# Raw weights loaded ahead, value products issued in blocks, and nine early tiles transposed on TensorE

## The chip, the core and the metric

The kernel runs on one core of a Trainium2 chip. Its engines work side by side, each through its own queue in order: TensorE (PE; its weight loads are listed as PEld), VectorE (DVE), ScalarE (ACT), GpSimd (POOL) and SyncE (SP), which here issues every DMA. The metric is the device time of one execution in microseconds (us); lower is better.

## The reference

The reference is attention in which a query only sees keys of its own cluster, and a feed-forward network behind it.

```
q, k, v: (4, 8, 768, 64)    centroids: (8, 16, 64)    out: (3072, 512), float32
q_assign = argmax(normalized q . normalized centroid)        # the same for k
mask     = q_assign[:, :, :, None] == k_assign[:, :, None, :]
scores   = where(mask, q @ k.T / sqrt(64), -1e9)
attn     = softmax(scores);   x = attn @ v  -> (3072, 512)
h        = max(x @ w1, x @ w2, x @ w3)                       # w: 512 x 768
out      = h @ w_out                                         # 768 x 512
```

The four weights come as float64, seen as pairs of 32-bit words, or as four 16-bit words each.

## The kernel before

**Precision.** Operands of the large matmuls are split into two float16 parts, high and low, and a product is the sum of three float16 products. Powers of two scale each operand first.

**Attention.** There are 4 batches, 8 heads in 4 pairs, and 6 tiles of 128 queries; 192 tiles of 128 queries x 768 keys in all, called steps here. A visit is one batch, one pair and three query tiles: six steps. `scores` does one step: four matmuls into a PSUM tile `big` (three buffers; L482 the product of q and k, L484 the cluster part), a minimum on DVE that also gives the row's extreme (L487), the exponential on ACT (L490), a cast to the high half (L493), a subtract for the low half (L495; on POOL at odd steps, on DVE at even ones), and a transposing DMA of both halves `hl` into `pt` (L496). After the six steps of a visit `av` multiplies by the values: it forms the reciprocals of the row sums, spreads them by small matmuls (L510) and makes 36 products of 64 columns (L514), two at a time side by side in the array, then scales and splits the result (L522 to L529).

**Preparation.** Before a pair's first step, `prep_units` loads q and k (L360), scales and splits them, finds the cluster of each row, and moves parts between partitions by DMA (L405 to L407, L463). `v_prep` scales (L330 in the first batch) and splits the values (L340, L341).

**Weights.** `w_units` (w1, w2, w3; six column blocks of three loads) and `wo_units` (w_out, six loads) bring in 24 raw pieces of 512 KB. In each, `convert` loads into one of two raw buffers `wd` (L195), casts the top 16 bits on ACT (L197) and merges the rest on DVE (L199). `hold` first writes one element of the raw buffer on POOL, out of the last step's row sum (L120), so the load can't start earlier. Maxima, scales (`pow2_scale`, L106) and the split (L208 to L210) follow.

**Feed-forward.** For each three query tiles of a batch, once all four pairs are there: `hidden` (18 units of 12 matmuls, L555) and `outp` (three units of 18 matmuls, L589).

**Order.** Every unit gets a priority, counted in steps; a scheduler that works with simulated times then sets each engine's order, taking what is ready with the lowest number. `spread` deals units over a stretch of steps; `behind` queues a unit behind the last instruction of a kind on its engine. Numbers below 0 in `W_LATE` and the like put a unit ahead of the step it is filed under.

## Time and profile before

| | |
|---|---|
| median of three runs | 871.94 us (867.68 to 874.14) |
| the profiled execution | 872.91 us, span 871.1 us |
| mean granted TensorE clock | 0.923 |
| busy: PE, DVE, ACT, POOL | 729.3, 559.7, 463.1, 450.4 us |
| DMA queue q1 | 71.5% of the 16 engines' span |
| transposing DMAs | 192, 4.0 us from issue to landing (median) |

A line such as `L495 POOL TENSOR_TENSOR hl<-e,hl` names the line of the kernel, the engine, the operation, and the tile written and those read. "x96 | 159.0, 1656" is the count, the busy time in us and the mean length in ns. A chain of waits is followed back from the last instruction, at each step to what released it. The granted clock is the share of full speed that TensorE had.

### The profile page before, as it was taken

To read this page: it belongs to the slowest core of one execution; us is meant where nothing else is said; L and a number is where in the kernel's file an instruction comes from. 1 tells how busy PE (TensorE), PEld (TensorE's weight loads), DVE (VectorE), ACT (ScalarE), POOL (GpSimd) and SP (SyncE) were. 2 spreads that over 40 slices of the span, in tenths; PEclk is the share of its full clock that TensorE was granted. 3 is DMA by queue.
4 is the path that set the end of the run, shared out by engine and by line. 5 is a ranking of instruction groups with operands and counts; after the bars stand their busy time and mean duration, and the time that the engine had idled before them with its cause. 6 is when DMAs were issued, how large, how long until landed. Compare 5 with 4: busy or idle time off the path is not lost.

```text
span 871.1 us, 13288 instructions
## 1 busy us (share of the span) xinstructions
PE 729.3 (84%) x4629; PEld 391.6 (45%) x4629; DVE 559.7 (64%) x1169; ACT 463.1 (53%) x827; POOL 450.4 (52%) x464
## 2 busy tenths in 40 slices
PE   2035374788868989999789999997999999999997
PEld 0012132344434545555444555454545554555563
DVE  7663877786897867547686686368768663556110
ACT  2545467654663646646554656464556465566201
POOL 1166355658585565337655745266666652354221
PEclk9976566689888999999999999999999999999999
DMA  6176869986786778768888978597986976666300
GB/s 230 36 169 140 201 143 214 203 182 139 178 204 128 171 167 154 138 117 165 170 157 201 188 139 142 113 180 144 189 194 128 156 136 134 112 118 110 91 1 36
DMA packets 329154, 128.90 MB, mean 148 GB/s; under 512 B 304384, under 2 KB 315520, under 8 KB 329088
## 3 DMA queue, kind: packets, MB, share of 16 engines
q1 hardware_dynamic: 329088, 128.06, 71.5%
q8 instruction: 36, 0.59, 0.3%
q14 instruction: 30, 0.25, 0.1%
HBM read 31.49 MB, written 6.29 MB: 43 GB/s over the span
## 4 chain that ended last, share of the span: by engine, by line
PE 45%; DVE 18%; POOL 11%; DMA 10%; issue 9%; ACT 5%; SPq 1%; POOLq 0%; DVEq 0%; ACTq 0%
PE one L555 17%; PE one L589 11%; PE big L514 7%; DVE big L487 4%; PE big L482 4%; PE big L484 3%; POOL hl L495 3%; DMA pt<-hl 2%; DMA stage<-in_qk_dram 2%; PE big L510 2%; DMA wd<-in_moe_w_dram 2%; DMA wd<-in_moe_w_out_dram 2%; POOL qk L399 2%; DMA stage<-in_v_dram 2%; DVE hl L495 2%
## 5 line engine op out<-in xcount | busy, mean ns | idle before, releaser
L487 DVE TENSOR_SCALAR_CACHE_REDUCE big<-big,nsc 128x768 f32<-128x768 f32 x192 | 194.2, 1017 | 78.3 <-PE big L484 77.1
L495 POOL TENSOR_TENSOR hl<-e,hl 128x768 f16<-128x768 f32 x96 | 159.0, 1656 | 148.9 <-ACT hl L493 147.3
L555 PE MATMUL one<-x,w16a 128*128 128x384 f16 x1152 | 208.1, 330 | 5.1 <-DVE vf_h L567 3.7
L490 ACT ACTIVATE big<-big,nm 128x768 f32<-128x768 f32 x96 | 83.8, 873 | 146.3 <-DVE big L487 130.9
L555 PEld LDWEIGHTS <-w16a 128*128 128x128 f16 x1152 | 111.1, 98 | 90.0 <-issue 21.1
L482 PE MATMUL big<-qk 128*128 128x512 f16 (+1 forms) x384 | 105.9, 357 | 48.5 <-DVE hl L495 14.0
L514 PE MATMUL big<-pt,v 128*64 128x384 f16 x1152 | 129.8, 341 | 2.4 <-DMA pt<-hl 2.4
L490 ACT ACTIVATE e<-big,nm 128x768 f32<-128x768 f32 x96 | 86.5, 901 | 71.3 <-DVE big L487 56.4
L495 DVE TENSOR_TENSOR hl<-big,hl 128x768 f16<-128x768 f32 x96 | 91.4, 952 | 41.8 <-ACT hl L493 39.6
L555 PE MATMUL one<-x,w16b 128*128 128x384 f16 x576 | 108.3, 340 | 6.7 <-DVE vf_h L567 5.2
L484 PE MATMUL big<-qk 96*128 96x512 f16 (+1 forms) x384 | 106.5, 357 | 6.9 <-DVE qk L465 4.3
L514 PEld LDWEIGHTS <-v 128*64 128x64 f16 x1152 | 71.8, 114 | 50.9 <-issue 26.0
L482 PEld LDWEIGHTS <-qk 128*128 128x128 f16 x384 | 35.6, 102 | 104.8 <-issue 67.2
L493 ACT CAST hl<-e 128x768 f16<-128x768 f32 x96 | 80.1, 834 | 2.4 <-DMA pt<-hl 0.6
L555 PEld LDWEIGHTS <-w16b 128*128 128x128 f16 x576 | 57.5, 101 | 51.3 <-issue 17.5
L493 ACT CAST hl<-big 128x768 f16<-128x768 f32 x96 | 76.6, 798 | 2.0
L528 POOL TENSOR_SCALAR x<-xs 128x384 f16<-128x384 f32 x32 | 16.4, 512 | 99.3 <-DVE xs L524 83.8
L484 PEld LDWEIGHTS <-qk 96*128 96x128 f16 x384 | 40.4, 105 | 40.0 <-issue 9.2
L589 PE MATMUL one<-wo,wf_h 128*128 128x512 f16 x216 | 56.0, 381 | 0.8 <-ACT o L598 0.8
L589 PE MATMUL one<-wo,vf_h 128*128 128x512 f16 x216 | 51.8, 380 | 2.7 <-DVE vf_h L567 2.4
L367 DVE TENSOR_REDUCE q_m<-stage 128x1 f32<-128x768 f32 x32 | 30.2, 948 | 33.9 <-DMA stage<-in_qk_dram 33.8
L399 POOL TENSOR_TENSOR qk<-stage,qk 128x768 f16<-128x768 f32 x30 | 49.6, 1667 | 3.1 <-ACT qk L398 2.9
(150 smaller groups left out, 892.5 us busy)
## 6 DMA issues: line engine op xcount, KB each, us to landing
stage<-in_qk_dram SPq DMA_DIRECT2D x32, 384.0 KB, 5.0
wd<-in_moe_w_dram SPq DMA_DIRECT2D x18, 512.0 KB, 4.8
out_dram<-o SPq DMA_DIRECT2D x24, 256.0 KB, 2.5
qk<-qk SPq DMA_DIRECT2D x15, 384.0 KB, 4.3
qk<-qk SPq DMA_DIRECT2D x30, 192.0 KB, 3.4
stage<-in_v_dram SPq DMA_DIRECT2D x12, 384.0 KB, 4.6
pt<-hl SPq DMA_TRANSPOSE x192, 4.0
wd<-in_moe_w_out_dram SPq DMA_DIRECT2D x6, 512.0 KB, 4.5
```

The source lines that it names most:

```text
L367: nc.vector.tensor_reduce(m2[:, i : i + 1], x, axis=AX.X, op=ALU.max, apply_absolute_value=True)
L399: last["lo"] = nc.gpsimd.tensor_tensor(t[:, AQ, i], x, t[:, BQ, i], op=ALU.subtract)
L482: nc.tensor.matmul(t[:, lo:hi], aq[:, qs], ak[:, lo:hi], start=True, stop=False)
L484: last["pe"] = nc.tensor.matmul(t[:, lo:hi], bq[0:K2, qs], bk[0:K2, lo:hi], start=False, stop=True)
L487: last["nm"] = nc.vector.tensor_scalar(e, e, nsc[b, h // 2], 3.0e38, op0=ALU.mult, op1=ALU.min, accum_out=nm)
L490: nc.scalar.activation(x, e, AF.Exp, bias=nm, scale=-1.0, accum_out=r)
L493: nc.scalar.copy(hl[:, 0, :], x)
L495: eng.tensor_tensor(hl[:, 1, :], x, hl[:, 0, :], op=ALU.subtract)
L510: nc.tensor.matmul(t[D * i : D * i + D, at : at + P], w, ident, start=True, stop=True)
L514: nc.tensor.matmul(t[D * i : D * i + D, 0:NB], v[:, i, kt, a], pts[i][:, :, c * QT + kt, :], start=(n == 0), stop=(n == len(parts) - 1),)
L555: nc.tensor.matmul(t[:, 0:NB], w16[jt // JA][:, jt % JA, wa, i, ct], x16[b, gi, ct][:, xa, :], start=(n == 0), stop=(n == 3 * CT - 1),)
L589: nc.tensor.matmul(t[:, 0:DM], h16[jt][:, ha, tt * P : (tt + 1) * P], wo16[0][:, jt, wa, :], start=(n == 0), stop=(n == 3 * JT - 1),)
```

## The change

It has four parts.

1. **Loads apart from conversions.** `convert` becomes `w_load` and `w_convert`. `pace` and `hold` go, and with them the POOL copies. The 24 pieces are dealt 1.9 steps apart: piece n is loaded at step k - 1 and converted at step k + 1, with k = 2 + 1.9 (n - 2); the first two are loaded ahead of step 0. Each such unit is queued behind the last L487, L490 and L496 on their engines. Before, 18 pieces were spread over steps 0 to 37 and six over 33 to 47, with load and conversion together.
2. **TensorE transposes.** At steps 0, 3, ..., 24 the transposing DMA gives way to twelve TensorE transposes through a float16 identity into two PSUM tiles `one`; ACT copies the high half's result into `pt`, DVE the low half's.
3. **Value products as blocks.** `av` is cut in three: the sums (`av_sums`), the 36 products, and the split (`x_split`). The products get a priority six steps below that of the other two.
4. **Preparation.** The first two values' loads stand ahead of step 0, apart from their maxima; pairs 2 and 3 of the first batch are prepared over steps 2 to 7 and 7 to 13 (before: 4 to 9 and 10 to 15).

```diff
-    def convert(wp, src, a, d):
-        n = d.shape[-1]
+    def w_load(wp, src, a, n):
         x = wp.tile([P, n + 1, 4], I16, tag="wd", name="wd", bufs=2)
-        hold(x[0:1, 0, 0:2].bitcast(F32))
         xf = x.rearrange("p n w -> p (n w)")
         nc.sync.dma_start(out=xf[:, 1 : 1 + 4 * n].rearrange("p (a m) -> p a m", a=a), in_=src)
+        return x
+
+    def w_convert(x, d):
+        n = d.shape[-1]
...
+        last["exp"] = nc.scalar.activation(x, e, AF.Exp, bias=nm, scale=-1.0, accum_out=r)
...
+        if not by_pe:
+            last["dma"] = nc.sync.dma_start_transpose(out=pt[:, g], in_=hl.rearrange("p a s -> p (a s)"))
+            return
+        for a in range(2):
+            o = one().bitcast(F16)[:, 0:S]
+            for c in range(QT):
+                nc.tensor.transpose(o[:, c * P : (c + 1) * P], hl[:, a, c * P : (c + 1) * P], identh)
+            d = pt[:, g, a * QT : (a + 1) * QT, :].rearrange("p c q -> p (c q)")
+            if a:
+                nc.vector.tensor_copy(d.bitcast(I16), o.bitcast(I16))
+            else:
+                nc.scalar.copy(d.bitcast(I16), o.bitcast(I16))
...
+    def paced(step, u, keys=("nm", "exp", "dma"), late=-2):
+        def f():
+            with ExitStack() as st:
+                for k in keys:
+                    if k in last:
+                        st.enter_context(tc.issue_after(last[k].ins))
+                u()
+        plan.setdefault(max(int(step // 1), 0), []).append((step + late, f))
...
+    W_STEP = 1.9
+    for n in range(24):
+        k = 2 + (n - 2) * W_STEP
+        if n >= 2:
+            paced(k - 1, (wl + ol)[n])
+        paced(max(k + 1, 0.5), (wc + oc)[n])
+        if n < 18 and n % 3 == 2:
+            for i, u in enumerate(wu[n // 3][2]):
+                paced(k + 2 + i, u)
+    paced(47, w_common)
+    spread([lambda u=u: behind("nm", u) for u in prep_units(0, 2)], 2, 7, -4)
+    spread([lambda u=u: behind("nm", u) for u in prep_units(0, 3)], 7, 13, -4)
...
-                at_prio(step, scores, b, h, gi * G + g, pt, g, rs, by_pool(step))
+                at_prio(step, scores, b, h, gi * G + g, pt, g, rs, by_pool(step), step < 26 and step % 3 == 0)
...
-        u = lambda a=(b, pr, gi, pts, rs): behind("pe", av, *a)
-        plan.setdefault(step + AV_LAG - 1, []).append((step + AV_LATE, u))
+        k = step + AV_LAG - 1
+        plan.setdefault(k, []).extend(
+            [
+                (k + 1, lambda a=(b, pr, gi, rs): behind("pe", av_sums, *a)),
+                (k - 5, lambda a=(b, pr, gi, pts): behind("pe", av, *a)),
+                (k + 1, lambda a=(b, pr, gi): x_split(*a)),
+            ]
+        )
```

How this moves instructions is seen on three engines. First TensorE about step 74, where the output matmuls of the first feed-forward block stand (`one<-wo,wf_h`), beside value products (`big<-pt,v`). Before:

```order
L510 MATMUL big<-ident,rs 64x128
L589 LDWEIGHTS wf_h
L589 MATMUL one<-wo_1015,wf_h 128x512
L514 LDWEIGHTS v_2390
L514 MATMUL big<-pt,v_2390 64x384
L589 LDWEIGHTS wf_h
L589 MATMUL one<-wo_1015,wf_h 128x512
L514 LDWEIGHTS v_2390
L514 MATMUL big<-pt,v_2390 64x384
```

After, where the products are L541, the output matmuls L619 and the row sums L533:

```order
L619 LDWEIGHTS wf_h
L619 MATMUL one<-wo_1156,wf_h 128x512
L533 MATMUL big<-ident,rs 64x128
L541 LDWEIGHTS v_2505
L541 MATMUL big<-pt,v_2505 64x384
L541 LDWEIGHTS v_2505
L541 MATMUL big<-pt,v_2505 64x384
L541 LDWEIGHTS v_2505
L541 MATMUL big<-pt,v_2505 64x384
```

Before, ten products alternate with output matmuls and 26 follow in a row; after, all 36 stand in a row.

Second ScalarE between the exponentials of steps 1 and 2 (`vf` and `v` are the values, `stage` and `qk` the q and k of the next pair). Before:

```order
L490 ACTIVATE e,rs<-big,nm 128x768
L493 CAST hl<-e 128x768
L330 ACTIVATE vf<-vf,s_v_301 128x768 x2
L397 ACTIVATE stage<-stage,q_s 128x768 x2
L330 ACTIVATE vf<-vf,s_v_301 128x768 x2
L340 CAST v_337<-vf 128x12x64
L340 CAST v_406<-vf 128x12x64
L398 CAST qk<-stage 128x768 x2
L340 CAST v_621<-vf 128x12x64
L340 CAST v_827<-vf 128x12x64
L490 ACTIVATE big,rs<-big,nm 128x768
```

After, with L503 for the exponential, L505 for the cast of the high half, L519 for the copy of a transposed tile, L195 for the cast of a raw weight, L410 and L411 for q and k:

```order
L503 ACTIVATE e,rs<-big,nm 128x768
L519 COPY pt<-one 128x768
L505 CAST hl<-e 128x768
L195 CAST top<-wd 128x512
L410 ACTIVATE stage<-stage,q_s 128x768 x2
L411 CAST qk<-stage 128x768 x2
L503 ACTIVATE big,rs<-big,nm 128x768
```

The eight instructions on the values have gone from here; they now stand behind step 4's.

Third POOL some steps later (`hl<-e` is the low half of an odd step, `wf` and `w16a` belong to the weights, `cl_t` to the clusters). Before:

```order
L120 COPY wd<-rs 1x1
L495 TENSOR_TENSOR hl<-e,hl 128x768
L440 TENSOR_TENSOR cl_t<-cl_t 128x24x16
L120 COPY wd<-rs 1x1
L445 TENSOR_TENSOR cl_t<-cl_t,cl_m 128x24x16
L528 TENSOR_SCALAR x_531<-xs 128x384
L529 TENSOR_TENSOR x_531<-xs,x_531 128x384
L120 COPY wd<-rs 1x1
L495 TENSOR_TENSOR hl<-e,hl 128x768 x2
```

After:

```order
L507 TENSOR_TENSOR hl<-e,hl 128x768
L208 TENSOR_TENSOR w16a<-wf,w16a 128x512
L453 TENSOR_TENSOR cl_t<-cl_t 128x24x16
L208 TENSOR_TENSOR w16a<-wf,w16a 128x512
L507 TENSOR_TENSOR hl<-e,hl 128x768
L458 TENSOR_TENSOR cl_t<-cl_t,cl_m 128x24x16
L507 TENSOR_TENSOR hl<-e,hl 128x768
L558 TENSOR_SCALAR x_602<-xs 128x384
L559 TENSOR_TENSOR x_602<-xs,x_602 128x384
```

The copies into `wd` are gone; the rest stands in a like order.

More of the change, by code (lines that the diff above doesn't have):

```diff
@@ L84 @@
     nc.gpsimd.tensor_copy(ident16, ident)
+    identh = cpool.tile([P, P], F16, name="identh")
+    nc.gpsimd.tensor_copy(identh, ident)
     rank = cpool.tile([P, C], F32, name="rank")
@@ L112, in pow2_scale @@
         return p, s
-    pace = []
-    def hold(x):
-        if pace:
-            nc.gpsimd.tensor_copy(x, pace[-1])
     last = {}
@@ L243, in split, with load, f @@
             return f
-        return [load(i) for i in range(3)] + [scale] + [split(i) for i in range(3)]
+        return [load(i) for i in range(3)], [conv(i) for i in range(3)], [scale] + [split(i) for i in range(3)]
     def wo_units(fp):
         got = []
+        raw = {}
+        def load(jt):
+            def f():
+                w = w_out.bitcast(I16)[jt * P : (jt + 1) * P, :]
+                raw[jt] = w_load(fp[0], w.rearrange("p (a n) -> p a n", a=1), 1, DM)
+            return f
         def part(jt):
             def f():
-                wp = fp[0]
-                w = w_out.bitcast(I16)[jt * P : (jt + 1) * P, :]
                 if jt % 3 == 0:
-                    got[:] = [wp.tile([P, 3 * DM], F32, tag="wf", name="wf", bufs=2)]
+                    got[:] = [fp[0].tile([P, 3 * DM], F32, tag="wf", name="wf", bufs=2)]
                 x = got[0][:, jt % 3 * DM : (jt % 3 + 1) * DM]
-                convert(wp, w.rearrange("p (a n) -> p a n", a=1), 1, x)
+                w_convert(raw.pop(jt), x)
                 row = worow[:, jt : jt + 1]
@@ L283, in common @@
             wsc["w"], wsc["o"] = pw, po
-        return [part(jt) for jt in range(JT)] + [common]
+        return [load(jt) for jt in range(JT)], [part(jt) for jt in range(JT)], common
     vmax = cpool.tile([P, B, NPAIR], F32, name="vmax")
@@ L308, in v_max_first, with load @@
     def v_max_first():
+        def load(i):
+            x = v_first[i] = fp[0].tile([P, 2 * S], F32, tag="vf", name="vf", bufs=2)
+            h = H // 2
+            nc.sync.dma_start(out=x, in_=vv[0, :, i * h : (i + 1) * h].rearrange("p h t d -> p (h t d)"))
         def part(i):
             def f():
-                x = v_first[i] = fp[0].tile([P, 2 * S], F32, tag="vf", name="vf", bufs=2)
-                h = H // 2
-                nc.sync.dma_start(out=x, in_=vv[0, :, i * h : (i + 1) * h].rearrange("p h t d -> p (h t d)"))
+                x = v_first[i]
                 nc.vector.tensor_reduce(
@@ L321, in sc @@
             vsc[0] = pow2_scale(vmax[:, 0, 0:2], "v0")
-        return [part(0), part(1), sc]
+        return [lambda: load(0), lambda: load(1), part(0), part(1), sc]
     v16 = {}
@@ L473, with scores @@
     SCALE = 1.0 / D**0.5
[L477 removed]
+    def scores(b, h, qt, pt, g, rs, by_pool, by_pe):
         aq, bq, bk, ak = (qkt[b, h // 2][:, j, h & 1] for j in range(4))
@@ L495, in scores, with av_sums @@
         eng.tensor_tensor(hl[:, 1, :], x, hl[:, 0, :], op=ALU.subtract)
-        last["dma"] = nc.sync.dma_start_transpose(out=pt[:, g], in_=hl.rearrange("p a s -> p (a s)"))
+        if not by_pe:
[10 more added lines that the diff above has]
+                nc.scalar.copy(d.bitcast(I16), o.bitcast(I16))
     x16 = {}
-    def av(b, pr, gi, pts, rs):
-        v = v16[b, pr]
-        t = big()
+    av_out = {}
+    def av_sums(b, pr, gi, rs):
+        t = av_out[b, pr, gi] = big()
         nc.scalar.activation(rs, rs, AF.Copy, bias=1.0e-9)
```

50 lines of the change are left out of this document (25 added, 25 removed).

## The prediction

> **What bounds the kernel now.** I read the page's head first, then the busy time by stage, then the chain of waits, then single stretches of TensorE's timeline.
>
> ```profile
> span 871.1 us, 13288 instructions
> PE 729.3 (84%) x4629; PEld 391.6 (45%) x4629; DVE 559.7 (64%) x1169; ACT 463.1 (53%) x827; POOL 450.4 (52%) x464
> ```
>
> The profiled execution took 872.9 us, its span is 871.1, so 1.8 us lie around it. It is 1.0 us above the median of the three runs, 871.9. TensorE is the fullest engine, but 84% is a mean over unlike stages. In the stage view the columns are the stretch, its length, busy time with instruction counts for PE, PE's weight loads, DVE, ACT and POOL, then the granted TensorE clock, the share of the DMA engines and GB/s:
>
> ```profile
> 0.00:65.00 65.00, 13.71 (x48) 5.04 (x49) 44.69 (x98) 28.18 (x45) 19.71 (x44) 0.92 0.55 146
> 65.00:109.00 44.00, 19.85 (x98) 8.69 (x99) 26.83 (x59) 22.40 (x38) 23.50 (x24) 0.58 0.75 169
> 109.00:183.00 74.00, 51.89 (x299) 26.72 (x299) 54.25 (x104) 50.91 (x92) 41.45 (x50) 0.67 0.90 193
> 183.00:257.00 74.00, 58.62 (x347) 31.96 (x346) 62.21 (x140) 40.99 (x72) 55.62 (x57) 0.88 0.76 168
> 257.00:452.00 195.00, 179.83 (x1183) 97.40 (x1183) 134.48 (x297) 105.68 (x191) 107.44 (x99) 0.97 0.78 153
> 452.00:636.00 184.00, 175.47 (x1158) 95.03 (x1158) 124.14 (x264) 106.33 (x194) 104.18 (x97) 0.98 0.81 161
> 636.00:805.00 169.00, 168.66 (x1139) 93.50 (x1138) 103.82 (x199) 99.29 (x182) 85.44 (x80) 1.00 0.73 136
> ```
>
> The first four rows hold the first 48 of the 192 score tiles ("steps"); the next three hold 48 each. From 257 us on TensorE is busy 92, 95 and nearly 100% of the time: there TensorE's own work is the bound. Before 257 us it is busy 144.1 of 257 us, at a clock of 0.58 to 0.92, and no engine is full: DVE has 188.0 us (44.69 + 26.83 + 54.25 + 62.21), the DMA engines reach 0.90 in one stage. So the front is bound by waits between engines. The chain of waits of those 257 us names them:
>
> ```profile
> by line: issue 10.5%; DMA wd<-in_moe_w_dram 6.4%; DMA wd<-in_moe_w_out_dram 6.2%; DVE big L487 4.8%; DVE wf L199 4.4%; DMA pt<-hl 4.0%; PE one L555 3.8%; POOL w16a L210 2.6%; DMA stage<-in_v_dram 2.5%; DVE q_m L367 2.4%; DMA qk<-qk 2.1%; PO
> ...
> 53.72 5.08 DMA wd<-in_moe_w_dram
> ...
> 242.21 6.15 DMA wd<-in_moe_w_out_dram
> ```
>
> Loads of raw weights (wd) are 6.4 + 6.2 = 12.6% of 257 us, 32.4 us in seven pieces, of which the first and the last stand above. In each the load has only just been issued when the cast that needs it comes up in ScalarE's queue (waited time, count, longest):
>
> ```profile
> ACT top L197 <- DMA wd<-in_moe_w_dram: 21.5, 12, 5.3
> ...
> ACT top L197 <- DMA wd<-in_moe_w_out_dram: 10.9, 5, 5.7
> ```
>
> **Raw weights ahead.** Before, load and conversion are one unit, and a one-element copy on POOL holds the load back. After, the plan puts the load two steps ahead of its cast. A step of the front lasts 257/48 = 5.4 us, so two last 10.7, and a load lands in 4.8 us at the median:
>
> ```profile
> wd<-in_moe_w_dram SPq DMA_DIRECT2D x18, 512.0 KB, 4.8
> pt<-hl SPq DMA_TRANSPOSE x192, 4.0
> L120 POOL COPY wd<-rs x22: 173/173/645, 52.0 to 238.6; 1x1 f32<-1x1 f32 x22
> ```
>
> So the 32.4 us of weight waits should leave the chain; the 22 POOL copies (22 x 0.17 = 3.8 us of POOL) go too, counted at nothing. The load now waits in the SP queue itself for one of two raw buffers, with the tile transposes queued behind it and, behind those, the value products. I price that at nothing: the conversion that frees the buffer is due 2.8 steps (15 us) earlier and is a cast and a merge of about 1 us each. Were this cover gone, each load would hold the queue for what the conversion is late, at worst the 4 to 6 us of a present piece.
>
> What is late next is DVE. It gets nine more copies, transposed tiles out of PSUM. The nearest row is its subtract over the same 128x768:
>
> ```profile
> L495 DVE TENSOR_TENSOR hl<-big,hl 128x768 f16<-128x768 f32 x96 | 91.4, 952 | 41.8 <-ACT hl L493 39.6
> L493 ACT CAST hl<-e 128x768 f16<-128x768 f32 x96 | 80.1, 834 | 2.4 <-DMA pt<-hl 0.6
> L495 POOL TENSOR_TENSOR hl<-e,hl 128x768 f16<-128x768 f32 x96 | 159.0, 1656 | 148.9 <-ACT hl L493 147.3
> L106 PE MATMUL one<-ident,sc_m 128*128 128x128 bf16 x20 | 4.8, 238 | 12.7 <-DVE sc_m L104 9.2 <-DVE vf_h L567 3.5
> ```
>
> 9 x 0.95 = 8.6 us, so DVE has 196.6 us to do. The fullest stage of the front shows DVE at 62.21/74 = 84%; at that share everywhere the front takes 196.6/0.84 = 234 us, 23 less than 257. The 32.4 us therefore do not all arrive: I take 23. The bounds are 0 (DVE, POOL and the preparation of q and k keep their gaps) and 32.4 + 10.3 (the 4.0% of waits for tile transposes as well).
>
> **Transposes on TensorE.** Steps 0, 3, ..., 24. Off the queues: 9 of 48 transposes of the front, each 4.0 us from issue to landing, in stages where the DMA engines are at 0.55 to 0.90. On TensorE: 9 x 12 = 108 matmuls of 128 columns; L106 gives at most 0.238 us each, 25.7 us in all, 2.9 a tile. TensorE is idle 97.5 of the first 183 us, so this is beside other work, unless it stands in the way: TensorE works in order, and the second six transposes of a tile wait for its low half, made by POOL (1.66 us) on four of the nine tiles and by DVE on five. The scores of the next steps stand behind. The order puts one or two steps' scores between a tile and its transposes, which hides most of it. I take 0.5 us a tile, 4.5 in all, between 0 and the full 0.83 + 1.66 + 2.86 = 5.4 us (cast, subtract, transposes) a tile. ScalarE's nine copies (9 x 0.83 = 7.5 us) lie in its 114.5 idle us of the front and count nothing; without that cover they cost those 7.5. The front: -23 + 5 = -18 us.
>
> The Trainium skill prices the transposes otherwise: "TensorE: Matmul & The Clock Gate", Part 4 (PE-mode transpose), has about 275 ns for one of 128x128 in a kernel; an estimate by it is 108 x 0.275 = 29.7 us, still less than the idle time, and the sum stays.
>
> The preparation of pairs 2 and 3 moves two to three steps earlier, and the scaling of the values on ScalarE and POOL moves from ahead of step 2 to behind step 4. The latter is now on the chain:
>
> ```profile
> 39.99 1.65 ACT vf L330 x2
> 41.64 0.73 ACT v L340
> 42.37 0.07 issue
> 42.44 2.18 POOL v L341 x2
> ```
>
> It must still be done before the first value products, so I count 0, between a gain of the 4.6 us shown and a loss of as much.
>
> **Value products in blocks.** In the late stages, where TensorE is the bound, the products L514 and the output matmuls L589 alternate. In this timeline the columns are start, length, instruction, count:
>
> ```profile
> 366.22 1.67 PE L589 MATMUL one<-wo,wf_h 128*128 128x512 f16 x7
> 367.83 0.43 PE L510 MATMUL big<-ident,rs 128*64 128x128 f32 x2
> ...
> 368.51 0.35 PE L514 MATMUL big<-pt,v 128*64 128x384 f16 x1
> 368.80 0.39 PE L589 MATMUL one<-wo,wf_h 128*128 128x512 f16 x1
> ...
> 374.53 2.30 PE L514 MATMUL big<-pt,v 128*64 128x384 f16 x26
> 376.77 0.34 PE L555 MATMUL one<-x,w16a 128*128 128x384 f16 x1
> ```
>
> Ten of each, alternating, take 374.53 - 368.51 = 6.02 us. Unmixed, seven L589 go from 366.22 to 367.83, 0.23 each, and 26 L514 from 374.53 to 376.77, 0.086 each: two products fill two halves of the array's columns (128*64) and run as a pair, and alternating breaks the pairs. Ten of each would take 3.16 us, so one alternation costs 0.286 us. Over the whole program the order has 50 places where an L514 follows an L589, all past step 48, and 4 after the change: 46 x 0.286 = 13.2 us. That is TensorE time where TensorE is full, so I count all of it, -13; the bounds are 0 and 13.2.
>
> The sum: 872.9 - 18 - 13 = 842 us for an execution like the profiled one, 841 against the median.
>
> **The rivals.** *Nothing in the front.* Preparation chains through DVE and POOL take over at once where the weight waits stood: 859 us. For it: in the fourth stage DVE is at 84% and POOL at 75%. Against: the first three stages are much emptier. 17%.
>
> *Transposes hold TensorE.* Scores queue behind a tile's low half and its twelve transposes; the full 5.4 us on nine tiles are 48 us, 872 - 31 + 48 = 889. It decides from 31/9 = 3.4 us beyond my sum a tile. For it: POOL's low half is the slowest piece of a tile (1.66 us). Against: at most three score tiles are in flight in PSUM, so scores far ahead could not have started anyway. 9%.
>
> *The clock stays up.* A fuller front raises the granted clock. 13.71, 19.85, 51.89 and 58.62 us of matmuls at 0.92, 0.58, 0.67 and 0.88 would be 110.5 at full clock, 33.6 less; half of it on the path is 17, so 824. For it: the clock is 1.00 where TensorE is full. Against: TensorE still idles nearly half of the front. 10%.
> The same part of that page of the Trainium skill says that transposes do not count as busy for the clock; by that rule 108 transposes would not help. No run here shows it yet.
>
> *Given back.* The front shortens, but a chain through the tile transposes, loads and POOL in the middle stages (DMA share 0.78 to 0.81) sets the pace and the time stays at 872. Against: TensorE at 92% and above there. 7%.
>
> **How the numbers follow.** My forecast has 57%: 841. About 1% (8.7 us) is what a measurement can tell from no change. Faster by more: 57 + 10 + 13 of the 17 of "nothing in the front" (859 is 1.5% off, near the line) = 80%; within 1%: 7 + 4 = 11%; slower: 9%. The range goes from 820, the clock's case with some more of the 10.3 us of transpose waits, to 864, the case with nothing in the front with some margin; what lies outside is the slower case, "given back" and little more.
>
> **What would show it.** In the changed profile the weight loads should be gone from the first 257 us' chain, and step 48 should start near 239 us, not 257 (wrong if above 252). DVE's share of the front should rise to about 80%. The alternating stretch should be one block of L514 of about 3 us; TensorE's busy time after the front should fall by some 13 us. If scores in the first 26 steps wait for low halves, or DVE and ScalarE wait for transposes, by more than 2 us a tile, the second rival is at work; a clock above 0.8 between 65 and 183 us would speak for the third.

## The result, and the profile after

The changed kernel takes 876.24 us (875.18 to 877.63), the kernel before in the same comparison 871.4 us (867.68 to 875.18). The ratio is 1.0056, with a 95% interval of 1.0040 to 1.0072: slower by half a per cent, where 841 us were predicted. Its profiled execution has a span of 874.9 us, against 871.1 before:

```profile
span 874.9 us, 13464 instructions
PE 726.0 (83%) x4737; PEld 402.7 (46%) x4737; DVE 564.1 (64%) x1178; ACT 466.2 (53%) x836; POOL 448.1 (51%) x443
```

TensorE does 108 matmuls more (the transposes) in 3.3 us less, and the span grows all the same: idle time is what increased. The stage view of the changed kernel, with the same columns as in the prediction; step 48 starts at 247.4 us (the start of the 49th minimum on DVE), and the last three rows hold 48 steps each:

```profile
0.00:65.00 65.00, 18.27 (x75) 8.04 (x75) 44.42 (x104) 31.08 (x48) 19.88 (x46) 0.83 0.52 150
65.00:109.00 44.00, 26.98 (x159) 14.16 (x160) 31.66 (x66) 27.84 (x49) 28.97 (x25) 0.66 0.71 167
109.00:183.00 74.00, 53.69 (x359) 30.88 (x356) 52.43 (x106) 48.78 (x87) 38.74 (x37) 0.77 0.72 158
183.00:247.40 64.40, 50.08 (x322) 28.89 (x321) 54.15 (x129) 39.08 (x70) 49.86 (x45) 0.92 0.78 170
247.40:444.30 196.90, 174.87 (x1159) 97.26 (x1159) 136.94 (x293) 105.04 (x192) 105.72 (x97) 0.95 0.76 152
444.30:635.50 191.20, 173.53 (x1158) 96.00 (x1158) 126.26 (x262) 104.46 (x191) 104.31 (x96) 0.97 0.79 153
635.50:808.60 173.10, 167.19 (x1152) 94.20 (x1151) 108.92 (x209) 100.47 (x185) 87.36 (x81) 0.99 0.75 136
```

The front did get shorter: 247.4 against 256.6 us, -9.2 where -18 was predicted. The three stages behind it got longer: 196.9, 191.2 and 173.1 us, against 195, 184 and 169 in the prediction's rows. TensorE, nearly 100% busy in the last of them before, is at 97%, and its granted clock is 0.95, 0.97 and 0.99 where it was 0.97, 0.98 and 1.00. The whole part behind step 48, before and then after, in one row each of the same view:

```profile
256.60:871.10 614.50, 585.20 (x3841) 319.15 (x3840) 372.08 (x776) 321.06 (x583) 310.56 (x293) 0.98 0.71 139
```

```profile
247.40:874.90 627.50, 576.98 (x3829) 320.76 (x3828) 381.49 (x778) 319.47 (x583) 310.64 (x291) 0.98 0.70 136
```

TensorE's busy time falls by 8.2 us (585.20 to 576.98). Its idle time, the length less the busy time, rises from 29.3 to 50.5 us. That is +13.0 us, where -13 was predicted. With the front's -9.2 it gives the +3.8 us of the spans.

In the front's chain of waits the loads of w_out are gone; those of w1 to w3 are down to 1.8%:

```profile
by line: PE one L585 6.6%; issue 5.6%; DVE big L500 4.1%; PE big L541 3.5%; DMA stage<-in_v_dram 2.5%; DMA pt<-hl 2.1%; DMA wd<-in_moe_w_dram 1.8%; ACT hl L505 1.8%; POOL qk L412 1.3%; ACT e L503 1.2%; PE big L495 1.2%; POOL hl L507 1.1%; D
```

ScalarE's waits for raw weights in the changed kernel (waited time, count, longest) are half of the 32.4 us of before, not nothing:

```profile
ACT top L195 <- DMA wd<-in_moe_w_dram: 13.4, 9, 3.0
...
ACT top L195 <- DMA wd<-in_moe_w_out_dram: 2.6, 1, 2.6
```

The transposes on TensorE (L514), DVE's copy (L517) and ScalarE's (L519), by line: durations as least/median/most in ns, and what ended TensorE's idle time ahead of them (that of the matmuls and that of the weight loads added up):

```profile
L514 PE MATMUL one<-identh,hl x108: 217/311/314, 26.0 to 151.7; 128*128 128x128 f16 x108
...
  ACT hl L505: 11.7, 6
  DVE q_m L383: 10.9, 2
...
L517 DVE COPY pt<-one x9: 544/552/559, 33.0 to 152.4; 128x768 int16<-128x768 int16 x9
...
L519 ACT COPY pt<-one x9: 785/792/815, 27.3 to 149.0; 128x768 int16<-128x768 int16 x9
```

The blocks are there as the order said: where ten products alternated with output matmuls about 370 us, 36 now take 3.3 us, from 364.9 to 368.2. The wait is seen better at a later block. TensorE around 433 us, in the changed kernel (start, length, instruction, count, idle before):

```profile
431.00 0.40 PE L440 MATMUL big<-qk,cw 128*64 128x512 f16 x1
433.14 2.14 PE L541 MATMUL big<-pt,v 128*64 128x384 f16 x24 [1.74 <-DMA pt<-hl]
...
438.73 0.49 PE L495 MATMUL big<-qk 128*128 128x512 f16 x2 [1.25 <-DVE cl_t L447]
...
440.68 0.48 PE L495 MATMUL big<-qk 128*128 128x512 f16 x2 [1.13 <-DVE xs L554]
```

24 products take 2.14 us, 0.089 each, the price of unmixed pairs. But TensorE stands still ahead of the block, for a transposing DMA whose result the products read, and twice behind it: three times in nine microseconds. ScalarE at the same place, in the same kernel:

```profile
431.11 0.80 ACT L505 CAST hl<-big 128x768 f16<-128x768 f32 x1
436.70 0.48 ACT L552 COPY xs<-big 128x384 f32<-128x384 f32 x1 [4.79 <-PE big L541]
```

Its copy of the row sums waits 4.79 us for the last product, with the next exponentials queued behind it.

### The profile page after: what moved, and what is told of

Same layout as the page of the kernel before. It is cut to its first block, busy times and chain, and to the rows that moved or that the text cites. A ratio compares the mean times of both kernels' runs of the same rounds, so it can differ in the third digit from the quotient of the medians.

```text
span 874.9 us, 13464 instructions
## 1 busy us (share of the span) xinstructions
PE 726.0 (83%) x4737; PEld 402.7 (46%) x4737; DVE 564.1 (64%) x1178; ACT 466.2 (53%) x836; POOL 448.1 (51%) x443
## 4 chain that ended last, share of the span: by engine, by line
PE 41%; DVE 13%; POOL 11%; issue 9%; DMA 6%; ACT 4%; SPq 1%; DVEq 0%; POOLq 0%; ACTq 0%
PE one L585 18%; PE one L619 8%; PE big L541 6%; DVE big L500 3%; PE big L495 3%; PE big L497 3%; POOL hl L507 3%; POOL qk L412 3%; DMA stage<-in_v_dram 2%; DMA stage<-in_qk_dram 2%; PE big L533 2%; POOL stage L408 1%; DVE hl L507 1%; ACT hl L505 1%; DMA pt<-hl 1%
## 5 line engine op out<-in xcount | busy, mean ns | idle before, releaser
L585 PE MATMUL one<-x,w16a 128*128 128x384 f16 x1152 | 209.2, 334 | 9.3 <-DVE vf_h L597 3.0
L503 ACT ACTIVATE big<-big,nm 128x768 f32<-128x768 f32 x96 | 84.0, 875 | 139.3 <-DVE big L500 122.6
L585 PEld LDWEIGHTS <-w16a 128*128 128x128 f16 x1152 | 112.7, 100 | 93.4 <-issue 25.7
L495 PE MATMUL big<-qk 128*128 128x512 f16 (+1 forms) x384 | 103.6, 354 | 45.8 <-ACT e L503 23.2
L503 ACT ACTIVATE e<-big,nm 128x768 f32<-128x768 f32 x96 | 86.7, 904 | 90.9 <-DVE big L500 82.3
L541 PE MATMUL big<-pt,v 128*64 128x384 f16 x1152 | 114.5, 334 | 7.4 <-DMA pt<-hl 7.4
L585 PE MATMUL one<-x,w16b 128*128 128x384 f16 x576 | 104.3, 332 | 1.7 <-DVE q_p L387 1.3
L541 PEld LDWEIGHTS <-v 128*64 128x64 f16 x1152 | 72.5, 112 | 39.7 <-issue 13.5
L505 ACT CAST hl<-e 128x768 f16<-128x768 f32 x96 | 80.2, 835 | 1.5
L505 ACT CAST hl<-big 128x768 f16<-128x768 f32 x96 | 76.6, 798 | 1.5
L585 PEld LDWEIGHTS <-w16b 128*128 128x128 f16 x576 | 56.6, 99 | 42.4 <-issue 7.5
L497 PEld LDWEIGHTS <-qk 96*128 96x128 f16 x384 | 40.0, 105 | 38.0 <-issue 10.2
L619 PE MATMUL one<-wo,vf_h 128*128 128x512 f16 x216 | 51.2, 389 | 6.5 <-DVE wo L292 5.5
L619 PE MATMUL one<-wo,wf_h 128*128 128x512 f16 x216 | 50.3, 379 | 0.8 <-ACT o L628 0.8
```

The lines of the kernel that those rows point to most:

```text
L495: nc.tensor.matmul(t[:, lo:hi], aq[:, qs], ak[:, lo:hi], start=True, stop=False)
L497: last["pe"] = nc.tensor.matmul(t[:, lo:hi], bq[0:K2, qs], bk[0:K2, lo:hi], start=False, stop=True)
L503: last["exp"] = nc.scalar.activation(x, e, AF.Exp, bias=nm, scale=-1.0, accum_out=r)
L505: nc.scalar.copy(hl[:, 0, :], x)
L541: nc.tensor.matmul(t[D * i : D * i + D, 0:NB], v[:, i, kt, a], pts[i][:, :, c * QT + kt, :], start=(n == 0), stop=(n == len(parts) - 1),)
L585: nc.tensor.matmul(t[:, 0:NB], w16[jt // JA][:, jt % JA, wa, i, ct], x16[b, gi, ct][:, xa, :], start=(n == 0), stop=(n == 3 * CT - 1),)
```

## The experiments

Every kernel is compared with the kernel before, run on the same chip; from comparison to comparison that one's median went from 870.6 to 873.5 us, so differences between experiments are taken from ratios, times 872 us. An interval of a ratio is 0.2 to 0.5% to either side; two ratios that differ by less than about 0.5% (4 us) are not told apart. In the tables, "step 48" is its start in the profiled execution, and "busy" and "idle" are TensorE's from there to the end, each from one row like the two above. They stand for one execution, whose time lies up to 4 us from the kernel's median, and how much work lies behind step 48 differs a little from kernel to kernel (3803 to 3841 matmuls); differences of two or three microseconds in these columns say little. "O-P" counts the places in the order where a value product follows an output matmul.

### The three parts, alone and together

The theories at the start: (1) the block saves TensorE time, and its late waits give it back; (2) the block's saving arrives, and the loss comes from the other parts.

Block alone in the kernel before:

```diff
-  plan.setdefault(step + AV_LAG - 1, []).append((step + AV_LATE, <av as one unit>))
+  k = step + AV_LAG - 1
+  plan: (k + 1, av_sums), (k - 5, av), (k + 1, x_split)
```

> The kernel before with the value products cut in three parts and their block ahead, nothing else changed. Theory 1 (the block saves TensorE's time, but waits that it makes in the late stages give it back): TensorE's busy time falls by 11 to 14 us, the time stays within 0.7% of before or is slower (866 to 882), and the late stages take at least as long as before. Theory 2 (the block's saving arrives, and what was lost comes from the other parts): about 858, 1.5% faster.

The loads alone (the changed kernel without the two other parts; the moved preparation, part 4 of the change, is in it):

```diff
-  at_prio(step, scores, ..., step < 26 and step % 3 == 0)
+  at_prio(step, scores, ..., False)
-  plan: (k + 1, av_sums), (k - 5, av), (k + 1, x_split)
+  plan: (k + 1, <sums, products and split as one unit>)
```

> The changed kernel with the value products in one unit as before and no TensorE transposes: raw weights ahead and the earlier preparation alone. Theory 1: the front gains, step 48 starts 5 to 12 us earlier than before, and the late stages are as before: 860 to 866. Theory 2: the front gains the same, but the late stages lose some 10 to 20 us: 870 to 885.

The transposes alone in the kernel before:

```diff
+  identh = <identity in float16>
   def scores(..., by_pool, by_pe):                 # by_pe: step < 26 and step % 3 == 0
-      last["dma"] = nc.sync.dma_start_transpose(out=pt[:, g], in_=...)
+      if not by_pe: <the same>
+      else: <per half: six transposes into PSUM, one copy into pt by ScalarE or DVE>
```

> The kernel before with nine tiles of the first 26 transposed on TensorE, nothing else. Theory 1: within 0.5% of before, since the chain of the front holds weight loads (12.6%) and few tile transposes (4.0%): 866 to 875. Rival (the transposes hold TensorE's queue): slower by 9 us or more, with scores in the first 26 steps waiting for low halves.

The changed kernel without the block (the second of the two edits above):

> The changed kernel with the value products in one unit as before: loads and transposes without blocks. Theory 1: step 48 starts near 247 as in the changed kernel, the late stages take 614 to 618 as before, 862 to 866 in all. Theory 2: 880 to 892, since the block's 13 us are missing.

The changed kernel without the transposes (the first of the two):

> The changed kernel without the TensorE transposes: loads ahead and blocks. Theory 1 (the blocks make the late stages' order depend on what came before; each order brings its own waits): the late stages again take another time than in the changed kernel (627 from step 48 to the end) and in the blocks-alone kernel (607), the whole anywhere from 850 to 878. Theory 3 (blocks and TensorE transposes disturb each other in the front, and what is lost late is their after-effect): about 851 to 855, the loads' 860 less the 5 that the blocks gain alone.

And, run later, the kernel before with transposes and block:

> The kernel before with the transposes on TensorE and the value products in blocks, loads as before: the last of the eight combinations of the three parts. If the parts add up, 885.4 (transposes alone) - 6 (the block's gain in the kernel before) = 879. If the block takes back what it saves whenever the front is disturbed (theory 2), as with the loads ahead (+7 without transposes, +15 with them), 892 to 900, with TensorE idle above 43 us after step 48. If the block's loss needs the loads ahead (a front ahead of the preparation), 876 to 881 and idle near 34 us.

| parts | time, us | ratio | 95% | step 48 | busy | idle | O-P |
|---|---|---|---|---|---|---|---|
| none (before) | 872 | 1 | | 256.6 | 585.2 | 29.3 | 50 |
| loads | 860.52 | 0.9845 | 0.981 to 0.988 | 244.8 | 581.3 | 34.0 | 41 |
| transposes | 885.40 | 1.0149 | 1.010 to 1.020 | 262.1 | 583.7 | 34.3 | 50 |
| block | 868.25 | 0.9930 | 0.991 to 0.995 | 256.4 | 572.8 | 34.2 | 6 |
| loads, transposes | 861.36 | 0.9860 | 0.982 to 0.990 | 248.3 | 579.7 | 30.0 | 42 |
| loads, block | 867.52 | 0.9947 | 0.993 to 0.997 | 239.6 | 573.6 | 53.7 | 5 |
| transposes, block | 878.91 | 1.0102 | 1.007 to 1.014 | 266.6 | 569.2 | 43.7 | 5 |
| all (after) | 876.24 | 1.0056 | 1.004 to 1.007 | 247.4 | 577.0 | 50.5 | 4 |

By themselves the loads (with the preparation) are worth most, -1.6%, and the block -0.7%. The transposes alone cost 1.5%; behind the loads they cost nothing that can be told (0.9860 against 0.9845). The block gains 6 us in the kernel before and 4 with the transposes (1.0102 against 1.0149, at the edge), but it costs 9 us behind the loads (0.9947 against 0.9845) and 17 behind loads and transposes (1.0056 against 0.9860). In every pair the block lowers TensorE's busy time, and in every pair the idle time rises: by 5, 20, 9 and 20 us. (Part of the two largest falls of busy time, 12.4 and 14.5 us in the pairs without the loads ahead, is that 13 and 33 matmuls fewer lie behind step 48.) Theory 1 stands as far as the place goes: the changed kernel without the block gains 1.4%, and the whole loss lies behind step 48.

### The block's price, and where it stands

The price first. Products a hundredth of a step ahead of the sums, just ahead of their tie with the output matmuls, so that they alternate more:

```diff
-  (k - 5, av)
+  (k + 0.99, av)
```

> The changed kernel with the products 0.01 of a step ahead of the sums: the order is that of the kernel without blocks but for more alternation, 71 places where a product follows an output matmul instead of 42. By my price of 0.286 us each: 29 x 0.286 = 8.3 us slower than without blocks (861), so 869, all of it in the late stages. Were alternation free where TensorE is full, it would stay at 861.

The part behind step 48 in the changed kernel without the block, and then in this one:

```profile
248.30:858.00 609.70, 579.68 (x3824) 317.66 (x3821) 374.14 (x768) 320.15 (x582) 307.96 (x289) 0.98 0.72 139
```

```profile
247.40:869.10 621.70, 589.53 (x3816) 320.58 (x3815) 372.64 (x770) 320.04 (x582) 308.33 (x289) 0.99 0.70 137
```

71 places where a product follows an output matmul against 42: 29 more, 9.85 us more busy time, 0.34 each where 0.286 was worked out. The part gets 12.0 us longer, idle time 2.15 us, and the time is 873.25 us (ratio 1.0014). So the price of an added alternation is about right, and TensorE time that is added costs all of itself. It is the way back that doesn't hold.

Next, whether it is the distance by which the products run ahead of the scores. Products half a step ahead of the tie, three steps ahead of it (six in the changed kernel), and a tenth of a step behind it, the last with and without the transposes:

```diff
-  (k - 5, av)
+  (k + 0.5, av)                                          # first
+  (k - 2, av)                                            # second
-  (k + 1, av_sums), (k - 5, av), (k + 1, x_split)
+  (k + 1.1, <sums, products and split as one unit>)      # third and fourth
```

> The changed kernel with the products half a step ahead of the sums, instead of six steps; 4 places remain where a product follows an output matmul, as in the changed kernel. Theory 1: TensorE's work is the same, the late stages differ from the changed kernel's 627 us by more than 5 us, in either direction. Theory 2 (a block that goes ahead of scores holds them back, so the priority sets the loss): clearly better than the changed kernel, 845 to 856, since products no longer pass scores that are due earlier.

> The changed kernel with the products three steps ahead of the sums (any number from two to five gives this same order). Theory 1: any of 850 to 880. Theory 2: between the half-step kernel and the changed kernel, 855 to 872.

> The changed kernel with each visit's sums, value products and split kept as one unit, 0.1 step later than in the version without blocks, so that the tie with the output matmuls is broken from behind instead of from six steps ahead. The order has 6 places where a product follows an output matmul (42 without blocks) and the blocks lie where they lay without them, to within a step. Theory 1 (being taken ahead of scores costs the fill, contiguous products cost nothing): TensorE's busy time after step 48 falls by 36 x 0.286 = 10 us against the version without blocks, its idle time stays near 30 us, and the time is 851 us (850 to 855). Theory 2 (a contiguous block itself makes the following stages wait, wherever it lies): idle time rises to 43 us or more, time 862 to 872. Theory 3 (any change of the order after step 48 away from the one without blocks costs something): between the two, 855 to 862.

> As the run before it, without the transposes on TensorE (loads ahead, products as one unit 0.1 step later). 4 places where a product follows an output matmul, 41 in the version with the loads alone. Theory 1: busy time after step 48 falls by 37 x 0.286 = 10.6 us against the loads alone, idle time stays near 34 us, time 850 us. Theory 2: idle time above 45 us, time 862 or more. In both theories the difference from the run before it is what the transposes on TensorE are worth in the front: within 3 us of nothing.

| products | time, us | ratio | 95% | step 48 | busy | idle | O-P |
|---|---|---|---|---|---|---|---|
| six steps ahead (after) | 876.24 | 1.0056 | 1.004 to 1.007 | 247.4 | 577.0 | 50.5 | 4 |
| three steps ahead | 870.45 | 0.9985 | 0.997 to 1.000 | 246.1 | 577.4 | 45.4 | 5 |
| half a step ahead | 870.37 | 0.9997 | 0.998 to 1.002 | 252.2 | 576.0 | 43.5 | 4 |
| a tenth behind | 857.98 | 0.9842 | 0.981 to 0.987 | 250.1 | 572.7 | 36.7 | 6 |
| in the tie (no block) | 861.36 | 0.9860 | 0.982 to 0.990 | 248.3 | 579.7 | 30.0 | 42 |
| a tenth behind, no transposes | 858.29 | 0.9839 | 0.981 to 0.987 | 243.9 | 573.7 | 39.2 | 4 |
| in the tie, no transposes | 860.52 | 0.9845 | 0.981 to 0.988 | 244.8 | 581.3 | 34.0 | 41 |

Ahead of the scores by whatever distance the block loses 1.2 to 2%; just behind the tie it loses nothing. That much of theory 1 of the run with the tenth is borne out: being taken ahead is what costs the time (the runs a tenth behind also keep sums, products and split in one unit; that was not varied alone). But its 851 us did not come. 7.0 and 7.7 us of busy time go, 0.19 and 0.21 for each of the 36 and 37 places where the price would have had 0.286; 6.7 and 5.3 us come back as idle time, and the gain over the version without a block (0.2% and 0.1%) can't be told from none. (The profiled execution with the transposes was the slowest of its six, 861.24 us, so some of its idle time may be its own.)

Part of the missing price is the clock. The trace's clock record knows two values, full and half speed. Behind step 48 it is at half for 30.0 to 41.4 us in the twelve kernels with at most six O-P places, and for 13.7 to 27.2 us in the eight with 40 or more. In the kernel a tenth behind, 25.6 us of matmuls fall into half speed, against 18.3 without the block. Matmuls one behind the other take about twice as long then: those of L585 end 162 ns apart at full speed and 320 at half (medians, in the changed kernel). By that, an estimate, the 7.3 us more at half speed cost 3.7 us of busy time; without them the 7.0 us would be 10.6, or 0.30 a place. Why the clock falls more often with blocks was not tried.

### ScalarE's hold

ScalarE's wait at the copy of the row sums (L552), from 250 to 805 us (waited time, count, longest), in the changed kernel and then in that without the block:

```profile
ACT xs L552 <- PE big L541: 40.0, 16, 5.4
```

```profile
ACT xs L552 <- PE big L541: 17.3, 14, 1.8
```

The other kernels with products half a step or more ahead, and the copy behind them, wait there 37 to 40 us, but for the block alone in the kernel before, 27.1; the two with products a tenth behind wait 16.6 and 20.4. First, the split of a visit's result two steps later:

```diff
-  (k + 1, x_split)
+  (k + 3, x_split)
```

> The changed kernel with only the split of a visit's result (ScalarE's copy out of PSUM, DVE's product and POOL's two halves) two steps later. Products stay where they are: 4 places where one follows an output matmul. Theory 1 (ScalarE, holding for the block with exponentials behind it, makes the late waits): ScalarE's wait for the products at that copy falls from 37 to 40 us to under 20 after 250 us, TensorE's idle time after step 48 from 50 to about 35, time 861 or less. Theory 2 (the late waits come from what the block no longer fills, not from ScalarE's hold): ScalarE's wait falls, TensorE's idle time stays at 45 to 50, time 872 to 878. Theory 3 (the block's PSUM buffer, held two steps longer, is missed by the scores): scores wait for a free buffer, time above 880.

This tested nothing: the instructions of all five engines come out in the order of the changed kernel. It measures the changed kernel a second time, on another chip: 876.86 us, ratio 1.0046, against 876.24 and 1.0056. Its profile has step 48 at 248.8 us and 48.1 us of idle time behind it, against 247.4 and 50.5: so far apart can two profiles of one order lie.

So the copy itself was moved: it reads only the sums, and is now issued between the sums and the products. In the changed kernel, in the version with the loads alone, and in the kernel before:

```diff
   def av_sums(...):           # in the last two: in av, between its two loops
       ...sums...
+      xs = ...; nc.scalar.copy(xs, t[:, 512 : 512 + NB])
   def x_split(...):
-      xs = ...; nc.scalar.copy(xs, t[:, 512 : 512 + NB])
```

> The changed kernel with ScalarE's copy of the row sums out of PSUM issued between the sums and the value products instead of behind the products; the products then wait for this copy. 1 place where a product follows an output matmul. Theory 1 (ScalarE's hold for the products, 40 us after 250 us in the changed kernel, makes the late waits): ScalarE's wait at that copy falls below 10 us, TensorE's idle time after step 48 from 50 to about 35 us, time 861 or less. Theory 2 (the loss lies in the order: products taken ahead no longer fill TensorE between scores): the wait at the copy falls, TensorE's idle time stays at 43 to 50 us, time 868 to 878. Theory 3 (products that wait for the copy hold TensorE in its turn): TensorE waits for the copy by more than 10 us, time 878 or more.

> The version with the loads alone (860.5), with the copy of the sums issued between the sums and the products; nothing else is put in blocks, but since the products wait for the copy they come behind the output matmuls: 5 places where one follows the other, 41 without. Theory 1: busy time after step 48 falls by 36 x 0.286 = 10.3 us and idle time stays near 34 us, 850 us. Theory 2: idle time rises by what the busy time falls, as in the changed kernel, 857 to 865. The version with the same products a tenth of a step later took 858.3, with 39 us idle: if ScalarE's hold was what it lost, this one is 3 us or more under it.

> The kernel before with only that copy issued between the sums and the products: 6 places where a product follows an output matmul, 50 before. Theory 1: 44 x 0.286 = 12.6 us of TensorE's time go and its idle time after step 48 stays near 29 us, 859 us. Theory 2: between the block alone in the kernel before (868) and 872. Step 48 stays near 256 us in both.

ScalarE's wait at that copy in the first of the three, over the same stretch:

```profile
ACT xs L537 <- PE big L535: 9.5, 9, 1.9
```

| copy ahead of the products | time, us | ratio | 95% | step 48 | busy | idle | O-P |
|---|---|---|---|---|---|---|---|
| changed kernel | 873.33 | 1.0008 | 0.999 to 1.003 | 247.9 | 577.9 | 41.7 | 1 |
| loads alone | 861.03 | 0.9874 | 0.984 to 0.991 | 238.6 | 578.6 | 40.7 | 5 |
| kernel before | 881.11 | 1.0099 | 1.007 to 1.013 | 259.7 | 578.4 | 41.7 | 6 |

In the changed kernel the wait falls from 40.0 to 9.5 us, idle time from 50.5 to 41.7 us, and 4 us of time are gained, at the edge of what can be told. The hold is real. Some 9 of the 21 us of new idle time go with it in the profile; since the profiled execution was the fastest of its twelve (869.31 us, median 873.33), the 4 us are the safer figure. What remains agrees with theory 2, which is not thereby shown. In the two other kernels the same edit also ends the alternation, since the products now wait for the copy: busy time falls by 2.8 and 6.8 us, idle time rises by 6.8 and 12.4, and the time is no better (0.9874 against 0.9845) or 1% worse. Theory 1's 850 and 859 us did not come.

Over all kernels run, the twelve with at most six O-P places idle 34.2 to 53.7 us behind step 48, and the eight with 40 or more 26.9 to 34.3 (three of these follow below).

### The loads

The loads alone bring 12 us at step 48, not 23. The chain of waits in the first 250 us of that version (start, length, what):

```profile
by line: issue 13.8%; DMA wd<-in_moe_w_dram 12.6%; DVE big L500 8.4%; DVE wf L197 4.2%; DVE hl L507 3.6%; DMA stage<-in_qk_dram 3.0%; DVE q_m L380 2.9%; ACT top L195 2.4%; POOL qk L412 2.4%; POOL v L354 2.2%; PE big L541 2.1%; DMA pt<-hl 1.
...
44.43 0.62 SPq L509
45.10 5.29 DMA wd<-in_moe_w_dram
```

Weight loads of w1 to w3 still are 12.6% of it, in six pieces, three of which start when the tile transpose (L509) ahead of them in the SP queue has been issued, as the one shown. ScalarE's waits there are 24.0 us, from 32.4:

```profile
ACT top L195 <- DMA wd<-in_moe_w_dram: 20.1, 11, 5.5
...
ACT top L195 <- DMA wd<-in_moe_w_out_dram: 3.9, 4, 2.0
```

Three ways to get a load out from behind the transposes: GpSimd's queue, ScalarE's queue, and one step more of lead on SyncE's:

```diff
-  nc.sync.dma_start(out=xf[...], in_=src)      # w_load
+  nc.gpsimd.dma_start(...)                     # first
+  nc.scalar.dma_start(...)                     # second
-  paced(k - 1, (wl + ol)[n])
+  paced(k - 2, (wl + ol)[n])                   # third
```

> The version with the loads alone (860.5; step 48 at 244.8) with the raw weight loads issued by GpSimd's queue instead of SyncE's; tile transposes stay on SyncE's. Theory A (tile transposes ahead of a load in the SP queue make it late, and the front loses what they cost): ScalarE's wait for raw weights falls from 24 us to below 10, step 48 starts at 233 to 239, time 849 to 855. Theory B (the wait falls, but the preparation of q and k and DVE take over): wait below 10, step 48 at 242 to 247, time 858 to 863. Theory C (the new queue is late in its turn, since GpSimd waits for casts and low halves): the wait stays at 20 or more, 858 to 866.

> The same with the raw weight loads issued by ScalarE's queue, ahead of the cast that needs them by two steps of ScalarE's own order. Theory A: as with GpSimd, wait below 10 us, step 48 at 233 to 239, 849 to 855. Theory B: wait below 10, step 48 at 242 to 247, 858 to 863. Theory C: ScalarE waits for DVE's maxima ahead of the issue, the lead is lost again, wait 20 us or more.

> The version with the loads alone, with the raw weight load planned three steps ahead of its cast instead of two, still on SyncE's queue. If the place in the plan is what makes it late: the wait for raw weights falls from 24 us to below 10, step 48 at 239 or earlier, time 855 or less. If a load that comes up early only waits in the queue for a raw buffer, with the tile transposes behind it (the cover that the prediction named): the wait falls, the transposes come later, step 48 stays at 244 to 250, time 859 to 866.

| loads alone, issued | time, us | ratio | 95% | step 48 | wait for weights | busy | idle |
|---|---|---|---|---|---|---|---|
| by SyncE, two steps ahead | 860.52 | 0.9845 | 0.981 to 0.988 | 244.8 | 24.0 | 581.3 | 34.0 |
| by GpSimd | 869.85 | 0.9973 | 0.995 to 1.000 | 248.9 | 1.0 | 586.7 | 31.0 |
| by ScalarE | 854.57 | 0.9803 | 0.976 to 0.985 | 240.6 | 0.8 | 585.0 | 26.9 |
| by SyncE, three steps ahead | 853.85 | 0.9786 | 0.974 to 0.983 | 242.8 | 8.4 | 580.5 | 28.0 |

ScalarE's remaining waits with three steps of lead:

```profile
ACT top L195 <- DMA wd<-in_moe_w_dram: 7.5, 3, 4.0
...
ACT top L195 <- DMA wd<-in_moe_w_out_dram: 0.9, 2, 0.6
```

From GpSimd the waits are gone and the gain too. The issues themselves take GpSimd's time, which the low halves and the preparation want. The order also has 50 O-P places instead of 41, but so has that with the loads from ScalarE, which is among the fastest: the places alone do not explain the loss. That GpSimd's time does was not isolated. By line, in that kernel:

```profile
L188 POOL DMA_DIRECT2D wd<-in_moe_w_dram x18 | 14.3, 797 | 37.6 <-issue 14.8 <-DVE wf L197 7.9 <-DVE wcol L234 4.6
```

An issue from ScalarE took 375 ns of its queue (median). From ScalarE, or a step earlier, the waits go, all but 0.8 and 8.4 us, and step 48 comes 4.2 and 2.0 us earlier. These two are the fastest kernels of the study, 2.0% and 2.1% under the kernel before and under the changed one by more; their lead over the loads as the change has them (0.4% and 0.6%) is at the edge of what can be told. With the loads from ScalarE the front is 16.0 us shorter than before (256.6 to 240.6); with those from GpSimd, and the waits as good as gone too, 7.7.

## Why the prediction was wrong

**The step that failed: "That is TensorE time where TensorE is full, so I count all of it, -13".** Behind step 48 the changed kernel has 8.2 us less of TensorE's work, not 13, and 21.2 us more of its idle time, which the prediction had at nothing: that part takes 13.0 us more, not 13 less. The price of an alternation was about right when alternations are added (0.34 us a place, against 0.286); taken away they gave less (0.19 and 0.21 in the two pairs with as many matmuls behind step 48 on either side, a tenth behind against in the tie), in part since more matmuls then ran at half speed. What does not follow above all is that the end moves by as much. A stage in which TensorE is 92 to 100% busy is one in which TensorE time that is added costs its full price (9.85 us of work, 12.0 us of length); it says nothing of how far the next chain behind it is when work is taken away. My reading is that this chain was as near as TensorE: of the 3 to 14 us of busy time by which the block's rows differ in the four pairs, at best 6 arrived (the block alone), and where the products run ahead of the scores of a shortened front, 9 to 17 us were lost. Three places where the time goes are seen. ScalarE holds at a copy until the last product, with exponentials behind it (40.0 us against 17.3); without that hold 4 us of time come back. The clock is at half speed for 30.7 us behind step 48 by the trace's record, against 20.6 before; TensorE is busy in 22.3 and 17.0 us of that, and the stage rows show it as 0.95, 0.97, 0.99 against 0.97, 0.98, 1.00. And DVE waits longer for loads of q and k: 36.7 us from 250 to 805 us, against 26.9 before and 27.7 in the changed kernel without the block. The two lines (before, changed kernel), and the one place where it stands for 8 us, with the next step's minimum behind it:

```profile
DVE q_m L367 <- DMA stage<-in_qk_dram: 26.9, 11, 3.3
```

```profile
DVE q_m L380 <- DMA stage<-in_qk_dram: 36.7, 14, 8.0
```

```profile
469.41 0.95 DVE L380 TENSOR_REDUCE q_m<-stage 128x1 f32<-128x768 f32 x1 [7.97 <-DMA stage<-in_qk_dram]
470.28 1.02 DVE L500 TENSOR_SCALAR_CACHE_REDUCE big<-big,nsc 128x768 f32<-128x768 f32 x1
```

How the rest of the idle time comes about, and why nearly every kernel with blocks idles more, also where the block stands just behind the tie and the hold is short, stays open. That products, when they lie between other matmuls, fill TensorE's gaps while the next scores are made ready fits all rows, but it was not isolated: no run changes the block without changing the rest of the order with it.

**Raw weights ahead, -23 in the front: half of it came, since a queue was counted at nothing.** "I price that at nothing" was said of the SP queue, for the wait for a raw buffer. That wait was small (SyncE waited 1.0 us at loads for a buffer in the first 250 us of the changed kernel), although the cover was less than was said: by the plan the conversion that frees a buffer is due 1.8 steps (10 us) ahead of the next load into it, not 2.8. What made the loads late was the queue's other side, the tile transposes ahead of a load: issued from ScalarE's queue, the loads left ScalarE 0.8 us of waits instead of 24.0. The loads alone brought 11.8 us at step 48, and issued from ScalarE 16.0; the rest of the 23 never came. The estimate by DVE's share (84% everywhere) was wrong too: the front settles at 182.66 us of DVE's work in 247.4, 74%, and at 179 of 240.6 in the version with loads from ScalarE. What bounds it there was not looked for.

**Transposes on TensorE, +4.5: near what was measured, in part by luck.** At step 48 they cost 3.5 us behind the loads, 5.5 in the kernel before, 7.8 beside loads and block and 10.2 beside the block alone. Its parts were off: DVE's copy took 0.552 us instead of 0.95, and a transpose 0.311 us at the median, not at most 0.238. But these lengths overlap: all 108 kept TensorE busy for 12.9 us, half of the 25.7 counted. What the Trainium skill gives in "TensorE: Matmul & The Clock Gate", Part 4 (PE-mode transpose), about 275 ns in a kernel, lies between the 217 and the 311 ns here. TensorE's matmuls idle 16.0 us ahead of the transposes, 5.5 of them for the tile's halves, 0.6 us a tile where 2 were named as the sign of "Transposes hold TensorE": that was not the case. Its 48 us did not come (its 889 us also counted the 4.5 us of the sum a second time). That the transposes alone cost 13 us (1.0149) was not foreseen; that is the time of the rival named ahead of that run (slower by 9 us or more), but not its wait: the matmuls idle 6.1 us for the halves there, 0.7 a tile. Step 48 explains 5.5 us of the 13, and 3.5 lie behind it, in a profile some 3 us faster than the median. What costs the rest was not looked for.

**Preparation and scaling moved, 0:** not tried apart; both are in every version with the loads ahead.

**The rivals.** "Given back" (872, 7%) named the right outcome: the front shortens and the stages behind it return it. But its chain was tile transposes, loads and POOL; what is seen is mostly the block's doing, and without the block nothing is given back (861). "The clock stays up" did not happen: it rose from 0.58 and 0.67 to 0.66 and 0.77 between 65 and 183 us, but not above the 0.8 named. "Nothing in the front" is refuted by step 48.

**What would show it.** Weight loads off the front's chain: nearly. Step 48 near 239: 247, short of "wrong if above 252" and still 8 us late. One block of about 3 us: 36 products in 3.3 us. TensorE's busy time down 13: 8. All of these speak of work, and none of them asked for the idle time behind step 48, where the loss was.

## What to carry to other kernels

A busy engine's share tells what added work costs there; what taken-away work is worth needs the distance to the next chain, and here, at 92 to 100% busy, it was 6 us at best and less than nothing at worst. Before a load is put ahead, look at what stands in its queue in front of it, not only at what it waits for: the same load, a step earlier or on another queue, was worth 4 to 5 us more, and from GpSimd it cost nearly the whole gain. Where a scheduler sets the order, try each part of a change alone and in pairs: here the loads alone were 1.6% faster and all three parts together 0.6% slower.

## What the runs showed of the hardware

- A 128x128 float16 transpose on TensorE, from start to end, took 217 ns at the least and 311 at the median, at a granted clock between 0.66 and 0.83 in the stages where they lie. By the trace's clock record, 31 of the 33 that started at full speed took 217 to 230 ns, and 57 of the 63 at half speed 311 to 314 (the other twelve lie ahead of its first entry, at 40 us). One behind the other they overlap: all 108 took 12.9 us.
- The copy of 128x768 16-bit values out of PSUM took 0.552 us on DVE and 0.792 on ScalarE, against 0.952 for DVE's float32 subtract over the same shape; priced from that row it was 0.4 us too dear.
- A weight load of 512 KB issued by GpSimd showed 797 ns of GpSimd's time for each of 18, 14.3 us, and one issued by ScalarE 375 ns of its queue; in the kernel with GpSimd's, most of the gain was gone.
- Beside 21 us more idle time behind step 48, the changed kernel had the clock at half speed for 10 us more (30.7 against 20.6), 5.3 of them with matmuls running (22.3 against 17.0).
